# Two elementwise products move from VectorE to GpSimd in a pre-LN transformer layer

## The chip, the cores and the metric

The kernel runs on one core of one Trainium2 chip. The metric is the device time of one execution in microseconds; the median of three runs is given, and the profile is of one further execution. The engines are named as the profile names them: PE is TensorE (matmuls; PEld its weight loads), ACT is ScalarE, DVE is VectorE, POOL is GpSimd, SP is the queue that issues the DMAs. SBUF is the on-chip memory with 128 partitions, PSUM the memory that matmuls write.

## The reference

A pre-LN layer over 2048 tokens of width 1024: attention with 32 heads of 32, then a feed-forward network with 3584 hidden columns and tanh-GELU. Inputs and output are bf16.

```python
def _A_ref(x, wqkv, wo):                      # H = 32, Dh = 32
    q, k, v = split_heads(x @ wqkv)
    p = softmax(q @ k^T * Dh ** -0.5)
    return merge_heads(p @ v) @ wo

def _B_ref(x, w1, b1, w2, b2):
    return gelu_tanh(x @ w1 + b1) @ w2 + b2

h  = x + _A_ref(layernorm(x), A_wqkv, A_wo)
h2 = h + _B_ref(layernorm(h), B_w1, B_b1, B_w2, B_b2)
```

(The reference's own code writes the same with einsum and transposes; B_x is not used.)

## The kernel before

**Jobs and rounds.** Attention is cut into 64 jobs: 8 blocks of 256 queries (qb) times 8 groups of four heads (g). A job has 8 rounds; a round takes 256 keys. In a round PE makes the scores of four heads (L805) in PSUM, ACT takes their exponentials in two instructions of 1024 columns into PT (L816, 1024 of them in all, of which 32 go to the spare buffers PX), and PE multiplies them with V (L842). For the softmax's denominators, DVE adds the two halves of the keys (L857, into PS, three buffers), and PE sums over partitions with a matrix of ones (L871). The scores have three pairs of PSUM banks that go round; everything else shares the two banks 6 and 7.

**The end of a job.** `Job.finish` runs on DVE: it transposes the denominators out of PSUM (L887), copies the output out of PSUM (L894), takes reciprocals of 8 columns (L897), spreads them by a second transpose (L898) and multiplies output and reciprocals, both f32 in the buffer OD (two of them), into OT, bf16 (L902). The job that comes last of all (`final`) does this product in two halves of 128 columns. OT is read by `wo`, the output projection.

**The stream.** While attention of later query blocks runs on ACT, PE and DVE also carry the rest of the layer for the earlier blocks, as background: for a unit u of 256 tokens `wo(u)`, `ln2(u)`, `ffn1(u)`, `ffn2(u)`. Units 0 to 6 are streamed like this; unit 7 comes after the last exponential, with its GELU on ACT. FFN1 of a streamed unit writes 14 banks; DVE adds the bias and puts them into gT (L1001), and after every second bank the function `gelu(u, k)`, k = 0 to 6, treats a piece of 1024 columns: with g the piece and w one of the two buffers uu, w = g*g (L1020, DVE), w + C2 (L1021, DVE), w*g (L1022, DVE), tanh (L1023, ACT), w + 1 (L1024, DVE), g = w*g (L1025, DVE). The factor one half is applied in FFN2's eviction (L1046). FFN2 of a unit starts when all of its gT is there.

**POOL.** GpSimd sets constants at the start and otherwise does four small steps of each layer norm (L622, L624, L626, L628), on one or two columns; DVE then normalises (L632), and in the stream a transposing DMA brings the result into hnT, which FFN1 reads.

**What sets the order.** The builder records tasks with the buffers they read and write, an assumed duration and a priority. `schedule` then plays the program through with these durations and writes down one fixed order for each engine; `assign` turns the remaining dependences into semaphore waits. On the chip each engine works through its list in order: an instruction whose inputs are late holds everything behind it on its engine. A changed engine or assumed duration of one task thus reorders all lists.

Of the kernel before, what the change touches and what calls it, by code (L numbers as in the profile page):

```python
# [8 lines left out]
ALU = mybir.AluOpType  # L9
# [328 lines left out]
def build_kernel(nc, A_x, A_wqkv, A_wo, B_w1, B_b1, B_w2, B_b2, out):  # L338
# [36 lines left out]
    def sb(area, name, shape, dtype, split=1, parts=1):  # L375


        off, n = area.take(shape, dtype)
        h = nc.alloc_sbuf_tensor_at(name, shape, dtype, offset=off)
        step = n // split  # L380
        bufs = []
        for i in range(split):
            ps = [gr.buf("SB", off + i * step, off + (i + 1) * step, (name, i)) for _ in range(parts)]
            bufs.append(ps if parts > 1 else ps[0])
        return h, (bufs if split > 1 else bufs[0])
# [33 lines left out]
    OT, B_OT_ = sb(top, "OT", [P, 3, G, 256], BF, 3 * G, 2)  # L419
    B_OT = [B_OT_[G * i:G * i + G] for i in range(3)]  # L420
    xrb, B_xrb = sb(ot_lo, "xrb", [P, 8, D], BF, 8)
    OD, B_OD_ = sb(top, "OD", [P, 2, 2, 256], F32, 4, 2)
# [9 lines left out]
    for k in range(6):  # L432
        h, b = sb(k_hi if k == 2 else ph0, "Wall%d" % k, [P, DC, 512], BF, 1, 4)
# [15 lines left out]
    uu, B_uu = sb(ffn, "uu", [P, NU, 1024], BF, NU)  # L449
    xq, B_xq = [], []  # L450
    for k in range(2):
        h, b = sb(xq_lo, "xq%d" % k, [P, DC, 512], BF)
# [69 lines left out]
    def c_dve_ps(n):  # L522
        return (120 + n) / 960.0 - 0.058

    def c_dve(n, x=1):
        return (62 + n / x) / 960.0
# [13 lines left out]
    def bi(bank):  # L540
        return bank.n if isinstance(bank, Slot) else bank
# [9 lines left out]
    def drop(t, bank):  # L551
        if isinstance(bank, Slot):
            t.rel = bank
# [21 lines left out]
    def act(fn, n, reads=(), writes=(), prio=0, ap_bias=False, kind="", after=()):  # L575
        return gr.add(E.Activation, fn, c_act(n, ap_bias), 0.16, reads, writes, prio, kind, after=after)

    def dve(fn, occ, reads=(), writes=(), prio=0, after=()):
        return gr.add(E.DVE, fn, occ, 0.135, reads, writes, prio, after=after)

    def pool(fn, occ, reads=(), writes=(), prio=0):
        return gr.add(E.Pool, fn, occ, 0.1, reads, writes, prio)
# [10 lines left out]
    def dma_transpose(out_ap, in_ap, nbytes, reads, writes, prio):  # L593
# [5 lines left out]
         reads=[B_ident], writes=[B_ident])  # L599
# [226 lines left out]
    class Job:  # L826
# [52 lines left out]
        def finish(self):  # L879
            qb, g, bank = self.qb, self.g, self.bank  # L880
            u = qb % 3
            o = cnt["od"] % 2
            cnt["od"] += 1
            B_O, B_D = B_OD[o]
            final = qb == 2 * NCH - 1 and g == G - 1
            D = OD[:, o, 1, :].rearrange("p (b j) -> p b j", j=32)
            t = dve(lambda v: v.transpose(OD[:, o, 1, :], psum[:, bi(bank), 256:512]), 0.36,  # L887
                    reads=[self.B_O, self.B_D], writes=B_D, prio=-1)
            drop(t, bank)
            if final:  # L890
                t = act(lambda a: a.activation(OD[:, o, 0, :], psum[:, bi(bank), 0:256], ACT.Copy), 256,
                        reads=[self.B_O, self.B_D], writes=B_O, prio=-1, after=[t])
            else:
                t = dve(lambda v: v.tensor_copy(OD[:, o, 0, :], psum[:, bi(bank), 0:256]), c_dve_ps(256),  # L894
                        reads=[self.B_O, self.B_D], writes=B_O, prio=-1)
            drop(t, bank)
            dve(lambda v: v.reciprocal(rr[:, o, :], D[:, :, 0]), 0.1, reads=B_D, writes=[B_rr[o]], prio=0)  # L897
            dve(lambda v: v.transpose(D, rr[:, o, :].unsqueeze(2).to_broadcast([P, 8, 32])), c_dve(256),  # L898
                reads=[B_rr[o]], writes=B_D, prio=0)
            for k in range(2 if final else 1):  # L900
                c = slice(128 * k, 128 * k + 128) if final else slice(0, 256)
                dve(lambda v, c=c: v.tensor_tensor(OT[:, u, g, c], OD[:, o, 0, c], OD[:, o, 1, c], ALU.mult), c_dve(c.stop - c.start),  # L902
                    reads=B_O + B_D, writes=B_OT[u][g][k:k + 1] if final else B_OT[u][g], prio=1)

    pending = []
# [77 lines left out]
    def ffn1(u, tail=False):  # L983
        R = R2 if tail else R1
        for blk in range(FC // 2):
            s = wblock(R, None, block=blk)
            bank = blk % 6 if tail else slot()
            for f in range(2):
                for dc in range(DC):
                    mm(bank, R.w1[:, s, dc, f * P:(f + 1) * P], hnT[:, dc, :], dc == 0, dc == DC - 1,  # L990
                       [R.B_w1[s]] + B_hnT, not tail, (256 * f, 256 * f + 256))
            evict1(u, 2 * blk, bank, tail)
            if not tail and blk % 2:
                gelu(u, blk // 2)
# [19 lines left out]
    def gelu(u, k):  # L1014
        i = cnt["uu"] % NU
        cnt["uu"] += 1
        b = B_gT[2 * k:2 * k + 2]
        g = gT[:, 4 * k:4 * k + 4, :].rearrange("p f c -> p (f c)")
        w = uu[:, i, :]
        dve(lambda v: v.tensor_tensor(w, g, g, ALU.mult), c_dve(1024, 2), reads=b, writes=[B_uu[i]], prio=1)  # L1020
        dve(lambda v: v.tensor_scalar(w, w, C2, None, ALU.add), c_dve(1024, 4), reads=[B_uu[i]], writes=[B_uu[i]], prio=1)  # L1021
        dve(lambda v: v.tensor_tensor(w, w, g, ALU.mult), c_dve(1024, 2), reads=b + [B_uu[i]], writes=[B_uu[i]], prio=1)  # L1022
        act(lambda a: a.activation(w, w, ACT.Tanh, bias=0.0, scale=KT2), 1024, reads=[B_uu[i]], writes=[B_uu[i]], prio=-1)  # L1023
        dve(lambda v: v.tensor_scalar(w, w, 1.0, None, ALU.add), c_dve(1024, 4), reads=[B_uu[i]], writes=[B_uu[i]], prio=1)  # L1024
        dve(lambda v: v.tensor_tensor(g, w, g, ALU.mult), c_dve(1024, 2), reads=b + [B_uu[i]], writes=b, prio=1)  # L1025

    def ffn2(u, j, wide=False, W=None, banks=None):
        R = R2 if wide else R1
# [34 lines left out]
    for k in range(80):  # L1063
        pe(lambda p: p.matmul(psum[:, 6, 0:256], ident[:, :], b2t[:, 0:256], start=True, stop=True), 0.18 if k < 42 else 0.115,
           reads=[B_ident, B_b2t], writes=[B_ps[6]], kind="warm")
# [274 lines left out]
```

## Time and profile before

| | |
|---|---|
| Median of three runs | 1077.47 us (1077.18 to 1079.19) |
| The profiled execution | 1078.62 us, span 1076.8 us |
| Exponentials, L816 into PT and PX | 922.8 + 31.3 us on ACT, 1024 instructions |
| tanh, L1023 | 57.1 us on ACT, 49 instructions of 1168 ns |
| Denominator sums, L857 reading PT | 285.3 us on DVE, 431 instructions of 686 ns |
| GELU on DVE, L1020, L1021, L1022, L1024 | 33.4, 20.4, 33.5, 20.3 us, 49 instructions each |
| Layer norm's steps on POOL, L622 to L628 | 25 of each, together under 49.3 us |
| Granted TensorE clock | 1.000 |

The span is the time from the first to the last instruction in the trace. A row of a group names line, engine and operation, what is written and read, shapes and count; then busy time and the mean length of one; then the engine's idle time in front of them. In a row of slices each digit is the busy share of one fortieth of the span in tenths. A row of the waits names who waited for whom, the total in us, how often, and the longest. A row of the timeline begins with start and length in us.

### The profile page before, as it was taken

The numbers are of one execution on the slowest core, as the hardware profiler recorded it, in microseconds if no ns is written. First come the engines' busy times: TensorE is split into PE (matmuls) and PEld (weight loads), VectorE is DVE, ScalarE is ACT, GpSimd is POOL, SyncE is SP. The second block draws the span as 40 slices with busy tenths as digits, with TensorE's granted clock in tenths as the row PEclk, the third lists the DMA queues.
The fourth block names the chain that finished last, engine by engine and source line by source line (L and its number), as shares of the span: only waits on it lengthen the run. The fifth ranks groups of instructions, "written<-read, shape, count | busy, mean of one in ns | idle before, by whom it ended". The sixth has DMA issues, their size and how long they took to land.

```text
span 1076.8 us, 41986 instructions
## 1 busy us (share of the span) xinstructions
PE 1042.2 (97%) x19117; PEld 610.0 (57%) x19184; DVE 750.6 (70%) x1438; ACT 1011.2 (94%) x1116; POOL 49.3 (5%) x110
## 2 busy tenths in 40 slices
PE   8999999999999999999999999999999999999998
PEld 6566555554444754574466457546644664565483
DVE  8767666665576896599479749867975897687501
ACT  4999999999999999999999999999999999999650
POOL 4200000000010001001000100000010001000100
DMA  8670544438464546654774655367447638976360
GB/s 214 171 186 21 153 138 120 139 119 295 165 186 129 187 169 205 212 191 145 229 239 166 207 206 189 125 212 268 147 152 247 216 131 274 303 229 211 136 243 19
DMA packets 136178, 196.38 MB, mean 182 GB/s; under 512 B 49216, under 2 KB 100288, under 8 KB 133184
## 3 DMA queue, kind: packets, MB, share of 16 engines
q1 hardware_dynamic: 136000, 193.70, 54.8%
q8 instruction: 150, 2.46, 0.9%
q14 instruction: 28, 0.23, 0.1%
HBM read 177.94 MB, written 27.26 MB: 191 GB/s over the span
## 4 chain that ended last, share of the span: by engine, by line
ACT 63%; PE 31%; DVE 3%; issue 1%; POOL 1%; DMA 1%; SPq 0%; DVEq 0%
ACT PT L816 57%; PE ps L568 8%; PE ps L565 7%; PE ps L571 6%; PE ps L805 5%; ACT uu L1023 4%; PE ps L842 3%; ACT PX L816 3%; PE ps L871 2%; DVE PS L857 1%; DVE st L617 1%; DMA xrb<-in_A_x_dram 1%; DVE hch L1046 0%; DVE gT L1025 0%; DVE xb L632 0%
## 5 line engine op out<-in xcount | busy, mean ns | idle before, releaser
L816 ACT ACTIVATE PT<-ps 128x1024 bf16<-128x1024 f32 x992 | 922.8, 1174 | 6.7 <-PE ps L805 6.6
L857 DVE TENSOR_TENSOR PS<-PT 128x1024 bf16<-128x1024 bf16 x431 | 285.3, 686 | 115.1 <-PE ps L871 65.2
L805 PE MATMUL ps<-QT,KT 32*128 32x256 bf16 x4096 | 203.9, 273 | 6.8 <-ACT PT L816 3.7
L842 PE MATMUL ps<-PT,V 128*32 128x256 bf16 x3968 | 175.4, 273 | 2.3 <-issue 1.3
L805 PEld LDWEIGHTS ps<-QT,KT 32*128 32x128 bf16 x4096 | 61.0, 92 | 164.9 <-ACT PT L816 148.2
L871 PE MATMUL ps<-PS,ones 128*32 128x256 bf16 x1756 | 123.0, 274 | 2.6 <-issue 1.7
L842 PEld LDWEIGHTS ps<-PT,V 128*32 128x32 bf16 x3968 | 101.6, 97 | 29.9 <-issue 10.4
L565 PE MATMUL ps<-a_w2r,gT 128*32 128x512 bf16 x1520 | 109.6, 381 | 0.3 <-DVE hch L1046 0.2
L565 PE MATMUL ps<-hnT,a_w1r 128*32 128x256 bf16 x2864 | 103.8, 274 | 3.9 <-DVE gT L1001 2.2
L568 PE MATMUL ps<-hnT,a_w1r 128*128 128x256 bf16 x852 | 104.4, 273 | 0.2
L568 PE MATMUL ps<-a_w2r,gT 128*128 128x512 bf16 x355 | 88.1, 380 | 4.2 <-issue 2.2
L568 PEld LDWEIGHTS ps<-hnT,a_w1r 128*128 128x128 bf16 x852 | 78.3, 98 | 22.4 <-issue 12.9
L565 PEld LDWEIGHTS ps<-hnT,a_w1r 128*32 128x32 bf16 x2864 | 71.6, 96 | 22.5 <-issue 18.6
L1001 DVE TENSOR_TENSOR gT<-ps,b1f 128x512 bf16<-128x512 f32 x98 | 67.4, 688 | 17.8 <-PE ps L565 13.3
L1046 DVE SCALAR_TENSOR_TENSOR hch<-ps,hch 128x512 bf16<-128x512 f32 x32 | 21.9, 684 | 76.5 <-PE ps L571 47.1
L568 PE MATMUL ps<-xnT,Wall 128*128 128x512 bf16 (+1 forms) x270 | 56.6, 345 | 2.3 <-issue 1.0
L871 PEld LDWEIGHTS ps<-PS,ones 128*32 128x32 bf16 x1756 | 46.7, 96 | 19.7 <-issue 6.8
L568 PEld LDWEIGHTS ps<-a_w2r,gT 128*128 128x128 bf16 x376 | 32.3, 98 | 43.9 <-issue 11.7
L1023 ACT ACTIVATE uu<-uu 128x1024 bf16<-128x1024 bf16 x49 | 57.1, 1168 | 0.0
L622 POOL CAST mvb<-mv 128x2 bf16<-128x2 f32 (+1 forms) x25 | 6.3, 252 | 966.4 <-DVE mv L619 966.4
L565 PEld LDWEIGHTS ps<-a_w2r,gT 128*32 128x32 bf16 x1520 | 34.5, 96 | 27.9 <-issue 16.6
L568 PE MATMUL ps<-wov,OT 128*128 128x512 bf16 x174 | 43.6, 380 | 1.8 <-DVE rr L897 0.8
(93 smaller groups left out, 1005.9 us busy)
## 6 DMA issues: line engine op xcount, KB each, us to landing
a_w2r<-w_blocks SPq DMA_DIRECT2D x105, 512.0 KB, 5.5
a_w1r<-w_blocks SPq DMA_DIRECT2D x98, 512.0 KB, 3.9
wov<-wo_blocks SPq DMA_DIRECT2D x16, 1024.0 KB, 4.9
w_blocks<-in_B_w_dram SPq DMA_DIRECT2D x28, 512.0 KB, 3.9
b_w1r<-w_blocks SPq DMA_DIRECT2D x14, 512.0 KB, 4.6
a_w1r<-in_A_wqkv_dram SPq DMA_DIRECT2D x11, 512.0 KB, 4.6
Wall<-in_A_wqkv_dram SPq DMA_DIRECT2D x17, 256.0 KB, 4.7
xrb<-in_A_x_dram SPq DMA_DIRECT2D x16, 256.0 KB, 5.1
```

What stands on the lines that cost most here:

```text
L565: fns.append(lambda p, j=j: p.matmul(psum[32 * j:32 * j + 32, bi(bank), c0:c1], lhsT[:, 32 * j:32 * j + 32], rhs, start=start, stop=stop, ...
L568: t.whole = lambda p: p.matmul(psum[:, bi(bank), c0:c1], lhsT, rhs, start=start, stop=stop, skip_group_check=True)
L571: t = pe(lambda p: p.matmul(psum[:, bi(bank), c0:c1], lhsT, rhs, start=start, stop=stop), occ, reads=reads, writes=[bb(bank)], mode="full" ...
L617: dve(lambda v, c=c, k=k, x_ap=x_ap: v.bn_stats(st_l[:, i + k, 6 * c:6 * c + 6], x_ap[:, 512 * c:512 * c + 512]), 0.595, reads=B_x if isin ...
L805: return p.matmul(psum[:, 2 * us[h // 2] + h % 2, 256 * i:256 * i + 256], KT[32 * h:32 * h + 32, g, k0:k0 + P], QT[32 * h:32 * h + 32, qs, :],
L816: act(lambda a, u=u, k=k: a.activation(PTs[s][:, k, :, :], psum[:, 2 * u:2 * u + 2, :], ACT.Exp, bias=0.0, scale=SCALE), 1024, reads=[B_ps ...
L842: fns.append(lambda p, i=i, h=h: p.matmul(psum[32 * h:32 * h + 32, bi(bank), 0:256], V[:, g, 2 * r + i, 32 * h:32 * h + 32], PTs[s][:, h / ...
L857: dve(lambda v: v.tensor_tensor(PS[:, n, :, :], pairs[:, :, 0:256], pairs[:, :, 256:512], ALU.add), c_dve(1024, 2), reads=B_PTs[s], writes ...
L871: fns.append(lambda p, h=h, rhs=rhs, i=i: p.matmul(psum[32 * h:32 * h + 32, bi(bank), 256:512], ones32[:, :], rhs, start=False, stop=last, ...
L1001: t = dve(lambda v: v.tensor_tensor(g[:, fc:fc + 2, :], psum[:, bi(bank), :].rearrange("p (f c) -> p f c", f=2), b1f[:, fc:fc + 2].unsquee ...
L1023: act(lambda a: a.activation(w, w, ACT.Tanh, bias=0.0, scale=KT2), 1024, reads=[B_uu[i]], writes=[B_uu[i]], prio=-1)
L1046: drop(dve(lambda v, hs=hs, bank=bank, half=half: v.scalar_tensor_tensor(hch[:, hs, c], psum[:, bi(bank), :], half, hch[:, hs, c], ALU.mul ...
```

## The change

Two products change engine. In `Job.finish` the product of output and reciprocals goes to POOL for all jobs but the final one, with an assumed duration of 0.9 us. In `gelu` the last product, w*g into gT, goes to POOL for the pieces k < 7, with an assumed duration of 2.6 us. What they read and write and their priority are as before. Lines after L902 move down by one, lines after the second edit by four.

```diff
@@ Job.finish
             for k in range(2 if final else 1):
                 c = slice(128 * k, 128 * k + 128) if final else slice(0, 256)
-                dve(lambda v, c=c: v.tensor_tensor(OT[:, u, g, c], OD[:, o, 0, c], OD[:, o, 1, c], ALU.mult), c_dve(c.stop - c.start),
+                e, d = (dve, c_dve(c.stop - c.start)) if final else (pool, 0.9)
+                e(lambda v, c=c: v.tensor_tensor(OT[:, u, g, c], OD[:, o, 0, c], OD[:, o, 1, c], ALU.mult), d,
                     reads=B_O + B_D, writes=B_OT[u][g][k:k + 1] if final else B_OT[u][g], prio=1)
@@ gelu
         dve(lambda v: v.tensor_scalar(w, w, 1.0, None, ALU.add), c_dve(1024, 4), reads=[B_uu[i]], writes=[B_uu[i]], prio=1)
-        dve(lambda v: v.tensor_tensor(g, w, g, ALU.mult), c_dve(1024, 2), reads=b + [B_uu[i]], writes=b, prio=1)
+        if k < 7:
+            pool(lambda v: v.tensor_tensor(g, w, g, ALU.mult), 2.6, reads=b + [B_uu[i]], writes=b, prio=1)
+        else:
+            dve(lambda v: v.tensor_tensor(g, w, g, ALU.mult), c_dve(1024, 2), reads=b + [B_uu[i]], writes=b, prio=1)
```

## The prediction

> **What bounds the kernel now.** I read the busy shares and the slices first, then the waits, then the stretches in which the feed-forward stream runs, and last the neighbours of the instructions that the change moves.
>
> ```profile
> PE 1042.2 (97%) x19117; PEld 610.0 (57%) x19184; DVE 750.6 (70%) x1438; ACT 1011.2 (94%) x1116; POOL 49.3 (5%) x110
> ...
> DVE  8767666665576896599479749867975897687501
> ACT  4999999999999999999999999999999999999650
> ```
>
> ACT is full in every slice from the second to the thirty-seventh. Between 66 and 1000 us it is busy 930.27 of 934 us, so 3.73 us is all that any relief of another engine could win there. The waits say how close the others follow:
>
> ```profile
> PEld ps L805 <- ACT PT L816: 148.2, 444, 1.0
> ...
> ACT PT L816 <- PE ps L805: 6.6, 6, 3.0
> ```
>
> The scores' weight loads wait for ACT 444 times, 0.33 us on average (148.2/444) and at most 1.0: PE leads ACT by that little. ACT waits for PE only six times. A stop of PE or DVE of about a microsecond therefore reaches ACT, and nothing later on ACT makes it up.
>
> DVE's 70% is an average of two kinds of stretch. I cut out the seven in which a unit's FFN1 pieces and GELU run (columns: length, then busy time of PE, PEld, DVE, ACT, POOL):
>
> ```profile
> 352.00:404.00 52.00, 50.77 (x1107) 33.45 (x1108) 47.62 (x91) 51.61 (x57) 0.00 (x0) 1.00 0.53 177
> 449.00:501.00 52.00, 50.55 (x1038) 33.23 (x1033) 47.36 (x90) 50.95 (x57) 0.85 (x3) 1.00 0.52 182
> ...
> sum 348.00, PE 336.81 PEld 223.97 DVE 316.41 ACT 344.50 POOL 1.16; mean PE 48.12 PEld 32.00 DVE 45.20 ACT 49.21 POOL 0.17
> ```
>
> There DVE is 91% busy (316.41/348) beside an ACT at 99%; in the stretches between them it is at about 61%. All 49 GELU pieces lie in these 348 us.
>
> **What is moved, and its price.**
>
> ```profile
> L1025 DVE TENSOR_TENSOR gT<-uu,gT 128x1024 bf16<-128x1024 bf16 x49 | 33.6, 685 | 0.1
> ...
> L902 DVE TENSOR_TENSOR OT<-OD 128x256 bf16<-128x256 f32 x63 | 26.4, 419 | 0.6
> ...
> L603 POOL MEMSET b2t<- 128x1024 bf16 x1 | 1.0, 951 | 0.0
> ```
>
> *Removed from DVE.* 49 products of L1025 and the 63 of L902 that are not the final job's (its two halves stay). The condition k < 7 holds for every piece, since a unit has pieces 0 to 6. Busy time falls by 33.6 + 26.4 = 60.0 us. Instructions of DVE overlap a little (three sums of L857 take 1.90 us together, so 0.605 each from start to start), so in the seven stretches the work falls by 49 x 0.605 = 29.6 us and, for the 20 outputs that lie there (8.37 us busy / 0.419), by 20 x 0.33 = 6.6 us: from 316.4 to 280.2 us. Nothing of this reaches the end by itself, because ACT covers it.
>
> *Added to POOL.* No product of this size runs on POOL in this trace. The nearest row is the memset of 1024 bf16, 951 ns, which only writes; the memset of 32 columns takes 124 ns, so a stream costs (951-124)/992 = 0.83 ns an element. A product has two streams to read and one to write. Two streams one behind the other are 0.1 + 2 x 0.85 = 1.8 us (the low end), three are 2.85 us (the high end); I take the middle, 2.3 us. The 256-column output is by the same rule 0.53 to 0.74 us; I take 0.65. POOL then has 49 x 2.3 + 63 x 0.65 = 154 us more, far from its span. The Trainium skill (GPSIMD Engine Reference, section Performance versus the Vector engine) gives about 2.6 cycles an element for a product of two tensors, so 1024 x 2.6 / 1.2 GHz = 2.2 us as an estimate; by it the 36 us of the sum below would be 34, and no run here shows it yet.
>
> *What it meets on the way to memory.* The layer norms put small POOL instructions beside DVE's work, and there the trace shows a conflict. First a norm's chain with DVE at statistics (L617), then the next chain behind DVE's sums (L857):
>
> ```profile
> 404.40 0.18 POOL L622 CAST mvb<-mv 128x2 bf16<-128x2 f32 x1 [94.01 <-DVE mv L619]
> 404.67 0.23 POOL L624 TENSOR_SCALAR tb<-mvb 128x1 bf16<-128x1 bf16 x1
> 404.98 0.57 POOL L626 TENSOR_TENSOR denb<-tb,cexp 128x1 bf16<-128x1 bf16 x1
> ...
> 406.13 0.63 POOL L622 CAST mvb<-mv 128x2 bf16<-128x2 f32 x1
> 406.85 0.55 POOL L624 TENSOR_SCALAR tb<-mvb 128x1 bf16<-128x1 bf16 x1
> 407.48 0.97 POOL L626 TENSOR_TENSOR denb<-tb,cexp 128x1 bf16<-128x1 bf16 x1
> ```
>
> ```profile
> 406.02 2.61 DVE L857 TENSOR_TENSOR PS<-PT 128x1024 bf16<-128x1024 bf16 x4 [0.17 <-PE ps L871]
> ```
>
> The same three instructions take 0.63, 0.55 and 0.97 us in place of 0.18, 0.23 and 0.57. The cast at 406.13 ends at 406.76, just after the first of the four sums (406.02 + 0.69 = 406.71), though the second has begun: POOL waits for DVE's reading to pause, slips in, and goes on. The same stands beside the other products of two SBUF tensors (L976: casts of 0.53 us) and the fast one-source op L632 (0.38 us). It does not stand beside DVE instructions that read PSUM (L966, L690) or take statistics (L617). So DVE's instructions fall in two classes here: those that exclude POOL's read, and the free ones. I infer that whoever excludes POOL is excluded by it while POOL reads. POOL's reads here are 1 to 4 elements long, too short to show that side: the four sums took 2.61 us against 0.69 + 3 x 0.605 = 2.51, 0.10 us more. With 1024 elements the hold would be the length of the product, 2.3 us.
>
> The Trainium skill (SBUF — State Buffer, section on SBUF's two separate sides) speaks against the change in the same sense: VectorE and GpSimd share a port pair as an exclusive lock, taken by whoever starts first for the whole instruction, while the other blocks. By that rule the forecast below stands as it is; the rows above agree for POOL's side (0.63 us for 0.18) and are silent on DVE's, and the opposite reading is the first rival.
>
> *The sum in the seven stretches.* Of the DVE work that stays, 198.3 us are of the excluding class (L857 90.6, L1020 33.4, L1021 20.4, L1022 33.5, L1024 20.3) and 109.2 us free (L1001 63.4, L966 11.7, L887, L894, L897 and L898 29.5, L617 and L619 4.6): 64.5% excludes. POOL holds for 49 x 2.3 + 20 x 0.65 = 125.7 us. With free instructions under it in their share, DVE stands still for 0.645 x 125.7 = 81.1 us and needs 280.2 + 81.1 = 361.3 us where it has 348. If it used every idle moment, the stretches would grow by 13.3 us (0.27 a piece); if the 31.6 us that it idles now stay idle, by 44.9 us (0.92 a piece). The compiled order of the changed kernel helps little: the instruction right behind the "+1" (L1025 there) is an excluding one for 33 of 49 pieces. One piece followed by hand:
>
> ```profile
> 768.68 0.43 DVE L1024 TENSOR_SCALAR uu<-uu 128x1024 bf16<-128x1024 bf16 x1
> ...
> 769.02 1.89 DVE L857 TENSOR_TENSOR PS<-PT 128x1024 bf16<-128x1024 bf16 x3
> ...
> 770.82 0.69 DVE L1025 TENSOR_TENSOR gT<-uu,gT 128x1024 bf16<-128x1024 bf16 x1
> ...
> 771.43 0.69 DVE L1022 TENSOR_TENSOR uu<-uu,gT 128x1024 bf16<-128x1024 bf16 x1
> ...
> 772.15 1.10 ACT L1023 ACTIVATE uu<-uu 128x1024 bf16<-128x1024 bf16 x1
> ```
>
> POOL gets in when the first sum ends, near 769.7, and holds to 772.05. The second sum starts then and not at 769.63, and L1022, with one product less before it, at 773.26 and not at 771.43: 1.8 us late. The tanh on ACT starts 0.03 us after L1022's end, so ACT stands 1.8 us, and all exponentials behind it. Pieces with DVE idle behind them lose nothing. I take 0.75 us a piece, above the middle of 0.27 and 0.92 for the sake of such pieces: 49 x 0.75 = 36 us. Outside the stretches the 43 outputs hold 0.645 x 0.65 = 0.42 us each where 0.33 was removed, under a DVE that idles over a third: nothing. The first 60 us and the end past 1012 us have no moved instruction that is waited for: nothing.
>
> With the product at 1.8 us (outputs 0.53) the same sum gives 0 to 27 us, with 2.85 us (0.74) 32 to 63 us. The profiled execution took 1078.62 us (span 1076.8), 1.15 above the median of the three runs, 1077.47; 1078.6 + 36 = 1114.6 there, and about **1113 us** for the median; own range 1090 to 1138.
>
> *Waits added.* A product now passes through POOL's queue; behind it stand the layer norm's four steps and the outputs. FFN2 reads a product no sooner than its unit's last piece, and most pieces stand tens of us before it, so a product 2 to 4 us late is covered; if that cover is gone, PE waits that long. The buffer uu (two of them) is held 2 us longer, against pieces mostly 3 to 9 us apart.
>
> **The rivals.**
>
> *POOL gives way* (other side: not slower). If POOL's read yields to DVE element by element, DVE is never held, loses 60 us of work, and only the products stretch, as the casts did, with nobody waiting. For it: the four sums lost only 0.10 us. Against: the reads were of 1 to 4 elements. It decides if DVE's sums stay at 0.69 us beside a product. Its price is bounded by ACT's 3.73 us of idle time and a little disorder: 1074 to 1079 us, about 1076.5.
>
> *The norm's chain behind the products.* DVE is not held, but POOL, in order, serves the norm after a unit's last product. Now that chain starts 1.4 us after the last "+1" (402.97 to 404.40); with 2.3 us of product ahead of it, and one or two more when it is stretched, it is 1 to 2.5 us late, and with it a_xb, its transposing DMA and FFN1's first matmuls, which stand in PE's order ahead of scores. Seven units: 7 to 17 us, 1085 to 1095.
>
> *The hold is longer*, the product at 4 us: 49 x 4 + 20 x 0.8 = 212 us, x 0.645 = 137, less the 68 us that DVE has free after the removal: 69 us, 1147.
>
> **How the numbers follow.** Within 0.2% (1075.3 to 1079.6) cannot be told from no change. Held DVE 0.62, POOL gives way 0.24, norm's chain 0.08, longer hold 0.06. Giving way is faster by over 0.2% in 9 of its 24 parts and the same in 15; the rest is slower: 0.09, 0.15, 0.76. The range 1077 to 1138 leaves out about half of giving way and the longest holds, some 2 in 10.
>
> **What would show it.** Right: products on POOL near 2.3 us; DVE's sums and GELU steps recorded longer than 0.69 us, or with new idle time in front, beside them; ACT idle for some tens of us between 350 and 985, before tanh and exponentials; no more of it between the stretches. Wrong: sums at 0.69 us throughout, DVE simply emptier, and ACT still at 99% in the seven stretches.

## The result and the profile after

The changed kernel takes 1129.72 us (median of 5, 1127.97 to 1133.82) against 1079.19 us for the kernel before (median of 5 on the same chips): ratio 1.0473, 95% interval 1.0453 to 1.0493, some 51 us slower, where 36 us and about 1113 us had been forecast. The profiled execution took 1128.73 us. Lines after L902 are one higher than before, those after the GELU four: the "+1" is now L1025, POOL's product L1027, its output L903, the tanh L1024.

Busy time and slices of the page after:

```profile
PE 1061.0 (94%) x18982; PEld 607.7 (54%) x18982; DVE 771.2 (68%) x1326; ACT 1017.1 (90%) x1116; POOL 217.9 (19%) x222
...
DVE  8676565665667984896488659857974886696500
ACT  5999999999999899989987998999899889989750
```

ACT is no longer full: from the fourteenth slice on (28.2 us each; the first GELU stretch begins near 351 us) it drops to 8 and 7 in every unit. DVE shows more busy time than before (771.2 against 750.6 us) though 60 us of products have left it. The groups say why (line, engine, operation, shapes and count; busy us, mean ns; idle time before). The first row is of the kernel before, the others are of the changed one:

```profile
L857 DVE TENSOR_TENSOR PS<-PT 128x1024 bf16<-128x1024 bf16 x431 | 285.3, 686 | 115.1 <-PE ps L871 65.2 <-ACT PT L816 46.6
...
L857 DVE TENSOR_TENSOR PS<-PT 128x1024 bf16<-128x1024 bf16 x431 | 316.7, 761 | 126.5 <-ACT PT L816 68.5 <-PE ps L871 55.9
L1002 DVE TENSOR_TENSOR gT<-ps,b1f 128x512 bf16<-128x512 f32 x98 | 66.9, 683 | 20.2 <-PE ps L565 14.2 <-PE ps L568 5.9
L1021 DVE TENSOR_TENSOR uu<-gT 128x1024 bf16<-128x1024 bf16 x49 | 45.0, 918 | 0.7
L1023 DVE TENSOR_TENSOR uu<-uu,gT 128x1024 bf16<-128x1024 bf16 x49 | 44.8, 914 | 1.0
L1022 DVE TENSOR_SCALAR uu<-uu 128x1024 bf16<-128x1024 bf16 x49 | 36.3, 741 | 0.6
```

The denominator sums grew from 285.3 to 316.7 us, the GELU steps L1021, L1022 and L1023 from 33.4, 20.4 and 33.5 to 45.0, 36.3 and 44.8. With 1.8 us on L1025 and 1.1 on L977 that is 73 us more for the same work, nearly all of it in the GELU stretches. The eviction from PSUM (L1002) is unchanged at 683 ns. POOL's side:

```profile
L1027 POOL TENSOR_TENSOR gT<-uu,gT 128x1024 bf16<-128x1024 bf16 x49 | 113.7, 2321 | 155.7 <-DVE uu L1025 155.7
L903 POOL TENSOR_TENSOR OT<-OD 128x256 bf16<-128x256 f32 x63 | 57.5, 912 | 584.9 <-DVE OD L898 584.9
```

One piece in the timeline (start, length in us):

```profile
389.78 0.42 DVE L1025 TENSOR_SCALAR uu<-uu 128x1024 bf16<-128x1024 bf16 x1
390.11 0.42 DVE L1022 TENSOR_SCALAR uu<-uu 128x1024 bf16<-128x1024 bf16 x1
390.28 2.23 POOL L1027 TENSOR_TENSOR gT<-uu,gT 128x1024 bf16<-128x1024 bf16 x1 [5.16 <-DVE uu L1025]
390.45 0.68 DVE L1002 TENSOR_TENSOR gT<-ps,b1f 128x512 bf16<-128x512 f32 x1
391.05 2.01 DVE L1023 TENSOR_TENSOR uu<-uu,gT 128x1024 bf16<-128x1024 bf16 x1
...
393.09 1.06 ACT L1024 ACTIVATE uu<-uu 128x1024 bf16<-128x1024 bf16 x1 [0.73 <-DVE uu L1023]
```

The eviction L1002 runs inside POOL's product at its usual 0.68 us. L1023, which reads two SBUF tensors, starts 0.77 us into the product, ends at 393.06, 0.55 us after the product's end (392.51), and is booked as 2.01 us of work instead of 0.69. The whole trace repeats this: of 36 sums and products of two SBUF tensors that start while POOL makes a GELU product, 34 end 0.55 us after POOL does (0.545 to 0.553), ten fast one-source copies end 0.28 us after it, and none of the 17 instructions there that read PSUM or take statistics is longer than usual. The tanh waits 0.73 us for it, and every exponential behind the tanh is as much later. So a held instruction shows as a long one, not as idle time. The Trainium skill (SBUF — State Buffer, section on SBUF's two separate sides) has the shared port pair as an exclusive lock for the whole instruction of whoever starts first; for the product this trace agrees on DVE's side too.

The waits of the whole run, and the seven GELU stretches (length, then busy PE, PEld, DVE, ACT, POOL):

```profile
PEld ps L805 <- ACT PT L816: 155.3, 419, 1.1
...
ACT uu L1024 <- DVE uu L1023: 34.4, 34, 1.7
...
ACT PT L816 <- PE ps L805: 15.9, 13, 3.0
```

```profile
351.00:406.00 55.00, 47.91 (x936) 31.71 (x937) 49.95 (x77) 48.82 (x53) 18.03 (x10) 1.00 0.41 144
...
556.00:620.00 64.00, 55.79 (x1111) 35.86 (x1113) 52.61 (x81) 54.10 (x58) 19.32 (x10) 0.95 0.44 162
...
sum 394.00, PE 345.14 PEld 225.23 DVE 345.14 ACT 348.81 POOL 129.07; mean PE 49.31 PEld 32.18 DVE 49.31 ACT 49.83 POOL 18.44
```

ACT now stands 394.0 - 348.8 = 45.2 us in these stretches, where it stood 3.5. Between them (288 us) it stands 3.8 us, where it stood 0.2, and the 320 exponentials before 313 us keep the old pace to 0.2 us, with 19 moved outputs among them. From 66 us to the last exponential ACT's idle time thus grows from 3.7 to 49.0 us, 45 of the 51 us. The other 5 us stand in its busy time (944.2 in place of 938.9 us for about the same instructions). The tanh's wait, which the profile before does not have, is 34.4 us; that of the exponentials for scores grew from 6.6 to 15.9.

### The profile page after: what moved, and what is told of

It is laid out like the page before. It is cut to its first block, busy times and chain, and to the rows that moved or that the text cites. A ratio compares the mean times of both kernels' runs of the same rounds, so it can differ in the third digit from the quotient of the medians.

```text
span 1126.9 us, 41715 instructions
## 1 busy us (share of the span) xinstructions
PE 1061.0 (94%) x18982; PEld 607.7 (54%) x18982; DVE 771.2 (68%) x1326; ACT 1017.1 (90%) x1116; POOL 217.9 (19%) x222
## 4 chain that ended last, share of the span: by engine, by line
PE 39%; ACT 38%; DVE 19%; issue 3%; POOL 1%; DMA 1%; POOLq 0%; DVEq 0%
ACT PT L816 35%; PE ps L568 11%; PE ps L565 8%; PE ps L805 6%; PE ps L571 6%; PE ps L842 4%; DVE PS L857 4%; DVE gT L1002 3%; DVE uu L1023 3%; DVE uu L1021 3%; PE ps L871 3%; DVE uu L1022 2%; ACT PX L816 2%; ACT uu L1024 2%; DVE uu L1025 1%
## 5 line engine op out<-in xcount | busy, mean ns | idle before, releaser
L816 ACT ACTIVATE PT<-ps 128x1024 bf16<-128x1024 f32 x992 | 919.0, 1137 | 17.6 <-PE ps L805 15.9
L857 DVE TENSOR_TENSOR PS<-PT 128x1024 bf16<-128x1024 bf16 x431 | 316.7, 761 | 126.5 <-ACT PT L816 68.5
L903 POOL TENSOR_TENSOR OT<-OD 128x256 bf16<-128x256 f32 x63 | 57.5, 912 | 584.9 <-DVE OD L898 584.9
L1027 POOL TENSOR_TENSOR gT<-uu,gT 128x1024 bf16<-128x1024 bf16 x49 | 113.7, 2321 | 155.7 <-DVE uu L1025 155.7
L871 PE MATMUL ps<-PS,ones 128*32 128x256 bf16 x1756 | 122.4, 274 | 1.3 <-DVE PS L857 0.6
L565 PE MATMUL ps<-hnT,a_w1r 128*32 128x256 bf16 x2736 | 96.9, 274 | 22.9 <-DVE gT L1002 20.4
L568 PE MATMUL ps<-hnT,a_w1r 128*128 128x256 bf16 x884 | 111.9, 277 | 3.3 <-DVE gT L1002 2.9
L568 PE MATMUL ps<-a_w2r,gT 128*128 128x512 bf16 x414 | 102.3, 381 | 1.9 <-DVE hch L967 0.9
L565 PE MATMUL ps<-a_w2r,gT 128*32 128x512 bf16 x1368 | 99.0, 381 | 0.4 <-DVE gT L1002 0.3
L1024 ACT ACTIVATE uu<-uu 128x1024 bf16<-128x1024 bf16 x49 | 52.3, 1068 | 34.5 <-DVE uu L1023 34.4
L1002 DVE TENSOR_TENSOR gT<-ps,b1f 128x512 bf16<-128x512 f32 x98 | 66.9, 683 | 20.2 <-PE ps L565 14.2
L568 PEld LDWEIGHTS ps<-a_w2r,gT 128*128 128x128 bf16 x414 | 35.8, 98 | 50.5 <-issue 11.6
L568 PE MATMUL ps<-xnT,Wall 128*128 128x512 bf16 (+1 forms) x286 | 60.2, 348 | 0.5 <-ACT xnT L645 0.2
L871 PEld LDWEIGHTS ps<-PS,ones 128*32 128x32 bf16 x1756 | 45.8, 96 | 21.2 <-issue 6.3
```

The source lines that it names most:

```text
L565: fns.append(lambda p, j=j: p.matmul(psum[32 * j:32 * j + 32, bi(bank), c0:c1], lhsT[:, 32 * j:32 * j + 32], rhs, start=start, stop=stop, ...
L568: t.whole = lambda p: p.matmul(psum[:, bi(bank), c0:c1], lhsT, rhs, start=start, stop=stop, skip_group_check=True)
L816: act(lambda a, u=u, k=k: a.activation(PTs[s][:, k, :, :], psum[:, 2 * u:2 * u + 2, :], ACT.Exp, bias=0.0, scale=SCALE), 1024, reads=[B_ps ...
L857: dve(lambda v: v.tensor_tensor(PS[:, n, :, :], pairs[:, :, 0:256], pairs[:, :, 256:512], ALU.add), c_dve(1024, 2), reads=B_PTs[s], writes ...
L871: fns.append(lambda p, h=h, rhs=rhs, i=i: p.matmul(psum[32 * h:32 * h + 32, bi(bank), 256:512], ones32[:, :], rhs, start=False, stop=last, ...
L1002: t = dve(lambda v: v.tensor_tensor(g[:, fc:fc + 2, :], psum[:, bi(bank), :].rearrange("p (f c) -> p f c", f=2), b1f[:, fc:fc + 2].unsquee ...
```

## The experiments

Each ratio is to the kernel before on the same chip.

**Which half.** `e1_gelu_alone` leaves the outputs on DVE, `e2_outputs_alone` the GELU products (the first edit below is e1's, the second e2's).

```diff
-                e, d = (dve, c_dve(c.stop - c.start)) if final else (pool, 0.9)
+                e, d = dve, c_dve(c.stop - c.start)
```
```diff
-        if k < 7:
+        if k < 0:
```

> Only the GELU products go to POOL; the 63 outputs stay on DVE. Theory H (a product on POOL holds DVE's instructions that read two SBUF tensors or copy fast, and the 2.1 to 2.5 us holds of the 49 products in the crowded stretches make the loss): nearly all of the loss stays, 1118 to 1130 us. Rival P (each part costs by its time on POOL: the outputs are 57.5 of 171 us, a third): a third of the 51 us comes back, about 1112 us.

> Only the 63 job outputs go to POOL; the GELU products stay on DVE. Theory H: most outputs lie where DVE idles over a third, their holds (0.7 us) take no more than DVE saves: 1076 to 1083 us. Rival P (by time on POOL): a third of the loss, about 1095 us.

e1: 1132.97 us, ratio 1.0501 (1.0476 to 1.0526), as slow as both together, a little above what H gave. e2: 1078.84 us, ratio 0.9997 (0.9985 to 1.0009). The whole loss is the GELU products'. The outputs do hold DVE (L857 has a mean of 701 ns in e2), but most lie where DVE idles, and the time does not show it; 26 us taken off DVE win nothing either.

**Order or hold.** `e3_no_reading` keeps the changed kernel's order on every engine, and POOL as long at work, without reading.

```diff
-            pool(lambda v: v.tensor_tensor(g, w, g, ALU.mult), 2.6, reads=b + [B_uu[i]], writes=b, prio=1)
+            pool([lambda v: v.memset(w, 1.0), lambda v: v.memset(g, 1.0)], 2.6, reads=b + [B_uu[i]], writes=b, prio=1)
...
+                    f = [lambda v: v.memset(OD[:, o, 0, :], 1.0), lambda v: v.memset(OT[:, u, g, :], 1.0)]
```

> The order of all engines is that of the changed kernel, but POOL reads nothing: in place of a GELU product it fills uu and gT with a constant (two writes of 0.95 us each, 1.9 us), in place of an output OD and OT (two writes of about 0.3 us); these products are left out of the result. Theory H: without POOL reading, DVE's sums are back at 0.69 us and the time at 1076 to 1085 us (a fast copy may still be held by a write). Rival O (the loss comes from the new order that the planner wrote, with products 2.6 us late, or from results that come late out of POOL): the time stays at 1120 to 1130 us.

1083.07 us, ratio 1.0037 (1.0024 to 1.0049). Its groups:

```profile
L857 DVE TENSOR_TENSOR PS<-PT 128x1024 bf16<-128x1024 bf16 x431 | 284.3, 685 | 134.1 <-PE ps L871 66.6 <-ACT PT L816 65.5
...
L1030 POOL MEMSET uu<- 128x1024 bf16 x49 | 48.7, 995 | 142.4 <-DVE uu L1028 142.4
L1030 POOL MEMSET gT<- 128x1024 bf16 x49 | 48.7, 994 | 0.0
...
L1025 DVE TENSOR_SCALAR uu<-uu 128x1024 bf16<-128x1024 bf16 x49 | 24.4, 499 | 0.6
```

By the trace ACT, DVE and PE keep the order of the changed kernel, and the sums are back at 685 ns beside 97 us of POOL's writing into uu and gT. That order with results that come some 2 us after the "+1" is within 0.4% of the kernel before, so neither the new order nor lateness of that size made the loss: POOL's reading products did. (The fills take away the reading together with the multiplying; this run does not tell the two apart.) Only the fast one-source copy (here L1025, w + C2) is still longer, 499 ns in the mean against some 420: the copies that start during a fill end 0.28 us after it, so a fill holds them too.

**Where the stop reaches ACT.** `e4_tanh_later` tells the planner that L1023 reaches ACT later.

```diff
-        dve(lambda v: v.tensor_tensor(w, w, g, ALU.mult), c_dve(1024, 2), ...)
+        t = dve(lambda v: v.tensor_tensor(w, w, g, ALU.mult), c_dve(1024, 2), ...)
+        t.lat = 2.0
```

> As the changed kernel, but the planner is told that the third polynomial step (L1023) reaches ACT 1.9 us later, so that the tanh stands later in ACT's list. Theory H with the tight tanh as the place where DVE's lateness reaches ACT: ACT's 34 us of waits for L1023 fall below 10 us, and the time to 1095 to 1108 us. Rival C (DVE as a whole is too slow in the stretches, and lateness reaches ACT by any path): the waits move to the scores and evictions, and the time stays above 1118 us.

1135.60 us, ratio 1.0514 (1.0486 to 1.0542): the time is in C's range and H's narrower form falls. The waits of ACT for L1023 are gone from the top of the list, and in their place stands:

```profile
ACT PT L816 <- PE ps L805: 47.9, 54, 3.9
```

The tight tanh was the nearest door, not the only one: closed, lateness comes through the scores. The weight loads and matmuls of L871, which stand in PE's list ahead of scores, wait 43 us for DVE's sums (26.8 + 16.5), in the kernel before 4.3. Part of it is another thing: the granted TensorE clock was 0.989 in this run and 0.997 in the changed kernel's, in seven and in two spells of 3.4 us at half. By an estimate from these shares, 0.011 x 1134, it took at most some 12 us of PE's time; without them the time would still be above 1118.

**Dose.** `e5_three_pieces` moves three of a unit's seven pieces (k < 3). `e6_four_quarters` and `e10_eight_eighths` cut each product into 4 and 8 instructions of POOL.

```diff
-            pool(lambda v: v.tensor_tensor(g, w, g, ALU.mult), 2.6, ...)
+            pool([lambda v, c=c: v.tensor_tensor(g[:, c:c + 256], w[:, c:c + 256], g[:, c:c + 256], ALU.mult) for c in range(0, 1024, 256)],
+                 2.6, ...)
```

> Dose by number: of each unit only the first three GELU pieces (21 of 49) go to POOL, the outputs as in the changed kernel. If each hold costs by itself (theory H, about 1.04 us a piece), 21/49 of the 51 us: 1100 us (1094 to 1106). Rival C (the stretch as a whole has room for DVE, and only what exceeds it costs): with 28 products fewer the room suffices, under 1088 us.

> The order is that of the changed kernel; POOL makes each GELU product in four instructions of 256 columns one behind the other, about 0.6 us each, 2.4 us in all. If a hold lasts one instruction and DVE gets in between them, a stop is at most 0.6 us and DVE's sums grow by less: held instructions near 1.2 us in place of 2.2, and if stops shorter than the lead of PE over ACT are free, 1085 to 1105 us. Rival S (the sum of the holds counts, however it is cut, or POOL does not let go between its instructions): 1125 us or more.

> As the four quarters, with eight instructions of 128 columns, about 0.43 us each alone. If what counts is a stop's length against the lead of PE over ACT, DVE's held sums grow by 0.4 us at most and the loss halves again, 1085 to 1097 us. Rival (the sum of the holds counts from here on, since POOL's overhead is paid eight times): 1103 to 1115 us.

e5: 1109.58 us, ratio 1.0266 (1.0234 to 1.0299), 29 us for 21 pieces, 1.4 each: not less than in proportion, so the stretch had no room that would swallow a part. It is above the range that H gave; why a piece costs more here than the 1.03 of the whole change is not shown. e6: 1106.82 us, ratio 1.0246 (1.0222 to 1.0270): the loss is about halved for the same products, just above H's range and far below S. A piece of e6:

```profile
362.36 0.69 DVE L1002 TENSOR_TENSOR gT<-ps,b1f 128x512 bf16<-128x512 f32 x1 [0.33 <-PE ps L568]
362.57 3.90 POOL L1027 TENSOR_TENSOR gT<-uu,gT 128x256 bf16<-128x256 bf16 x4
362.96 0.82 DVE L857 TENSOR_TENSOR PS<-PT 128x1024 bf16<-128x1024 bf16 x1
363.70 1.16 DVE L1021 TENSOR_TENSOR uu<-gT 128x1024 bf16<-128x1024 bf16 x1
364.78 1.15 DVE L857 TENSOR_TENSOR PS<-PT 128x1024 bf16<-128x1024 bf16 x1
```

POOL and DVE take turns: each of the three DVE instructions that read two SBUF tensors waits for a quarter, and POOL waits for DVE between its quarters. It needs 3.90 us for what takes it 2.1 to 2.5 in one go. e10: 1100.43 us, ratio 1.0208 (1.0184 to 1.0232), hardly under e6 (the intervals overlap), between the ranges of H and of the rival. Cutting helps once; which of the two bounds the rest, length of a stop or POOL's overhead (392 instructions, 227.9 us), is not settled, and in e10 L1021 also waits 7.2 us until POOL's product gives back a buffer uu.

**The order that knows of the hold.** `e7_planned_hold` has the planner reckon DVE as taken for 2.1 us after the "+1".

```diff
-        dve(lambda v: v.tensor_scalar(w, w, 1.0, None, ALU.add), c_dve(1024, 4), ...)
+        t = dve(lambda v: v.tensor_scalar(w, w, 1.0, None, ALU.add), c_dve(1024, 4), ...)
+        t.occ += 2.1
+        t.lat -= 2.1
```

Here `occ` is the time for which the planner takes the engine, `lat` the time from then until the result is there.

> As the changed kernel, but the planner reckons DVE as taken for 2.1 us after each +1, as the hold takes it; POOL's product is planned at the same moment as before. Theory H with the order as the reason why no stop is absorbed (PE and ACT stand where the plan saw an idle DVE): ACT's waits for L1023 and for scores fall to a few us, and the time to 1085 to 1105 us, the rest being the DVE time that the holds cost. Rival C (the DVE time itself is the loss, whatever the order): 1120 us or more.

1109.34 us, ratio 1.0273 (1.0242 to 1.0303), between the ranges of H and C: neither held as it stood. ACT's slices:

```profile
ACT  4999999999999999999999999999999999995240
```

ACT is full again up to its last exponentials; the last exponential begins at 1005.8 us (1008.6 in the kernel before, 1059.2 in the changed one). But 100.8 us follow it in place of 68.2: feed-forward work slid behind the stream. In this kernel the hold was paid in one coin or the other, as stops of ACT or as work that comes too late. `e9_quarters_planned` joins the quarters with a smaller reckoning (1.0 in place of 2.1).

> The four quarters, and the planner reckons DVE as taken for 1.0 us (not 2.1) after each +1. In the run with 2.1 us the last exponential began at 1005.8 us, 2.8 us before that of the kernel before, and the loss lay in a tail longer by 33 us: feed-forward work had slid behind the stream. Theory H2 (a hold costs what the plan does not cover as ACT stops, and what it covers as work that slides; the sum falls with the length of a stop): last exponential below 1020 us, tail below 80 us, time 1082 to 1100 us. Rival (cutting and planning save the same loss, not each its part): 1105 us as for either alone.

1102.14 us, ratio 1.0215 (1.0197 to 1.0234), just over H2's range, its interval overlapping that of e6: the last exponential begins at 1030.2 us, later than H2's 1020, and 69.8 us follow it, as H2 has it. This cannot be told apart from cutting alone.

**The hold by itself.** `e11_useless_pass` takes nothing off DVE, and nobody reads what POOL makes. `e8_plus_one_on_pool` moves the one-source step w + 1 in place of the product. Both start from the kernel before.

```diff
         dve(lambda v: v.tensor_tensor(g, w, g, ALU.mult), ...)
+        pool(lambda v: v.tensor_tensor(w, w, w, ALU.mult), 2.6, reads=[B_uu[i]], writes=[B_uu[i]], prio=1)    # e11
```
```diff
-        dve(lambda v: v.tensor_scalar(w, w, 1.0, None, ALU.add), c_dve(1024, 4), ...)
+        pool(lambda v: v.tensor_scalar(w, w, 1.0, None, ALU.add), 1.2, ...)                                   # e8
```

> The kernel before, in which DVE makes all products, and beside it POOL squares the buffer uu in place after each GELU piece, 49 times, 1024 columns; the result is read by nobody. It prices the hold with nothing taken off DVE and no result that is waited for. Theory H: sums recorded at up to 2.7 us as in the changed kernel, and more than its loss, since DVE keeps the products: 1128 to 1160 us. Rival (the loss comes from products that POOL delivers late): 1076 to 1082 us.

> The kernel before, with another step moved: w + 1 (one tensor read, 0.42 us on DVE) goes to POOL, the products and outputs stay on DVE. It asks whether POOL holds DVE when it reads one stream alone. Theory H (any long read of POOL holds): the step takes about 1.0 us on POOL, sums of L857 that start beside it are recorded 0.3 to 1 us longer, and the time is 1079 to 1095 us. Rival T (only products of two tensors hold): sums stay at 0.69 us, 1076 to 1080 us.

e11: 1126.62 us, ratio 1.0457 (1.0433 to 1.0482), just under the foot of H's range and far from the rival's.

```profile
L857 DVE TENSOR_TENSOR PS<-PT 128x1024 bf16<-128x1024 bf16 x431 | 310.1, 746 | 89.0 <-ACT PT L816 46.9 <-PE ps L871 39.7
...
L1026 POOL TENSOR_TENSOR uu<-uu 128x1024 bf16<-128x1024 bf16 x49 | 102.3, 2088 | 538.0 <-DVE gT L1025 538.0
```

49 passes that no result depends on cost as much as the change (the planner's order differs from that of the kernel before here too; e3 is the run that keeps the order). That keeping the products on DVE made it no worse was not expected. It does not price the relief of DVE by itself, since POOL's passes, which read one buffer, are shorter here: 102.3 us in place of 113.7.

e8: 1115.07 us, ratio 1.0315 (1.0286 to 1.0344), outside both ranges. Two things are mixed in it. The step takes 2.94 us on POOL in the mean, where the planner was told 1.2 and the expectation had 1.0, and DVE stands 25.5 us for it ahead of the product; and it holds:

```profile
380.59 2.77 POOL L1024 TENSOR_SCALAR uu<-uu 128x1024 bf16<-128x1024 bf16 x1 [1.01 <-ACT uu L1023]
380.83 1.35 DVE L857 TENSOR_TENSOR PS<-PT 128x1024 bf16<-128x1024 bf16 x1
```

The sum ends at 382.18; taking off the 0.55 us that a held sum still needs after its release, it was let go near 381.6, 1.0 us into an instruction of 2.77. All 26 held sums and products of two SBUF tensors in this run end before POOL's instruction does, 1.19 to 1.35 us before it. So reading one stream holds too, but the hold ends before the instruction does; rival T falls.

No version beat the kernel before; e2 equals it.

## Why the prediction was right, and where its size was off

- *What bounds the kernel.* Right. ACT's idle time between 66 us and the last exponential was 3.7 us, and relief of DVE could not win more: e2 gives 26 us of relief for 0.9997.
- *The product's price on POOL.* 2.3 us from the memset's stream; measured 2.32, 2.12 where DVE did not hold it up. The middle of two bounds hit by some luck: no row of the profile before fixed it. The output was put at 0.65 and takes 0.91 (0.72 to 0.73 alone); as e2 loses nothing, that did not matter.
- *What it meets.* Right: the step that was only inferred, that DVE's instructions of the excluding class stand still while POOL reads, is shown by 2.01 us in place of 0.69, by the 44 held instructions that end just behind a product, by e3 (no reading, 685 ns) and by e11. The classes were right too: PSUM evictions ran inside the hold.
- *DVE's stop.* Put at 81.1 us in the stretches, measured there as about 72.
- *The cost of a piece* is the term that was mis-sized. The prediction had 0.27 us if DVE used every idle moment, 0.92 if none, and took 0.75, so 36 us. Measured is 50.5/49 = 1.03, and the stretches alone grew by 46 us, 0.94 a piece. That is above the bound: with the measured stop of 72 us the same sum gives 280.2 + 72 - 348 = 4 us if all idle time is used and 36 if none, and the same choice between them about 28. A stop put too high thus hid part of an absorption put too high. DVE idles 394.0 - 345.1 = 48.9 us in the stretches now, where it was 31.6. The sum treated DVE as if it were the bound, with a store of free time; but ACT waits for the instruction that is held (34.4 us for L1023 alone), and a stop of DVE is lost for ACT at once where PE and ACT follow within a microsecond. e4 shows that it does not depend on the one tight wait that the piece worked by hand showed, and e5 that fewer holds do not fall into free room. How the 1.03 is made up over the pieces is not shown.
- *Outside the stretches nothing.* Nearly right: ACT idles 3.8 us between them, where it idled 0.2, and e2 loses nothing.
- *The rivals.* POOL giving way falls with the 2.01 us. The norm's chain behind the products: DVE's wait for POOL ahead of a_xb rose from 1.5 to 3.2 us in all, and e3 has the same order without loss. The longer hold falls with 2.32 us.

## What to carry to other kernels

In these runs an elementwise step that GpSimd took off VectorE still stopped VectorE, wherever VectorE's next instruction read two SBUF tensors or was a fast copy: for the whole of a product of two tensors, and for about 1.0 us of the 2.77 of a one-source step. So look what stands there before moving such a step, and count GpSimd's length, not the share that is freed. Where engines wait for one another within a microsecond, as here, do not count on idle time elsewhere in a stretch to absorb a stop. If such a step has to move, put it where VectorE idles (the outputs cost nothing) or beside instructions that read PSUM (never held in these traces, though no run planned for it), and cut it into a few instructions (half the loss here).

## What the runs showed of the hardware that was not expected

A held instruction is booked as busy: DVE's busy time rose by 20.6 us when 60 us of work left it. Writing alone (97 us of fills) leaves sums of two tensors at 685 ns, but holds a fast copy that starts during a fill to 0.28 us after the fill's end (499 ns in the mean in place of some 420). A one-source w + 1 of 1024 columns takes POOL 2.77 us, longer than the two-source product (2.12), and holds DVE for about 1.0 us of it; here the Trainium skill's page on SBUF (SBUF — State Buffer, section on SBUF's two separate sides), by which the pair is held for the whole instruction, differs from the measurement, and the measurement decides. A product of 256 columns takes 0.66 us alone and one of 1024 2.12, so 1.9 ns a column and 0.2 us besides. POOL gets its turn between two DVE instructions that follow each other without a gap, and DVE between two of POOL's. In one stretch of the changed kernel (556 to 620 us) the granted clock of TensorE was 0.95, from two spells of 3.4 us at half, where the kernel before has none. Over the run that is at most some 3 of the 51 us, an estimate from 0.003 x 1127; whether the stops of PE bring the spells about was not tried.
